# Transposes in halves that yield on VectorE, and other planned durations, in a list-scheduled attention and mixer kernel

## The chip, the cores and the metric

The kernel runs on one core of one Trainium2 chip. The metric is the device time of one execution in microseconds (us). A profiled execution is taken apart by engine: PE is TensorE's matmuls, PEld its weight loads, DVE VectorE, ACT ScalarE, POOL GpSimd, SP SyncE. Times quoted from a trace count from the first instruction of the program.

Each comparison below was made on one chip with the kernel before run in between. A ratio is the mean time of one kernel's fast runs over the mean of the other's fast runs of the same rounds, so it isn't quite the ratio of the medians that stand beside it. "Fast" and "slow" are states of a run; the slow one has a lower mean granted TensorE clock.

## The reference

Block-causal attention (blocks of 64) over 8 batches and 8 heads of 576 x 64, then an MLP mixer on its output:

```python
def _attn_ref(q, k, v):                       # q, k, v: 8 x 8 x 576 x 64, float32
    scores = scale * np.matmul(q, k.transpose(0, 1, 3, 2))
    mask = block_i >= block_j                 # blocks of 64 rows and columns
    ...                                       # masked softmax
    return np.matmul(attn, v)

def _moe_ref(x, w_tok1, w_tok2, w_ch1, w_ch2):  # x: 8 x 576 x 512
    xt = x.transpose(0, 2, 1)
    h = np.maximum(xt @ w_tok1, 0.0) @ w_tok2   # 576 -> 256 -> 576
    u = x + h.transpose(0, 2, 1)
    h2 = np.maximum(u @ w_ch1, 0.0) @ w_ch2     # 512 -> 1536 -> 512
    return u + h2
```

## The kernel before

Every piece of work is an `Op` with an engine, a planned cost, dependencies and a priority. When the program is built, a list scheduler plays all engines against a clock of planned costs and fixes the order of instructions on each engine. On the chip the order stays; only the waits are real. The choice of the next op:

```python
for e in ("PE", "ACT", "DVE", "POOL", "SP"):
    ...
    if best is None or (-o.urgent, o.prio, o.n) < (-best.urgent, best.prio, best.n):
        best = o
    ...
    soon = t + 0.6 * o.cost[e]
    if any(r < soon and self.ops[n].urgent > o.urgent and e in self.ops[n].engines for r, n in queued) or ...:
        continue          # a more urgent op is about to be ready: leave the engine idle for it
    ...
    if o.xfer is not None:                     # a DMA
        first = o.end + self.FIRST[e]
        if e == "POOL":
            soft = max(soft, hard, first) + o.xfer
        else:
            hard = max(hard, first) + o.xfer
```

q and k of four heads are loaded with a cast to bf16 and transposed on VectorE in 32 x 32 blocks; the ring of raw buffers is three deep, so a transpose also sets when a later load may start:

```python
parts = ((0, NB // 2), (NB // 2, NB)) if b < 2 else ((0, NB),)
...
loads = [P.add("POOL", 0.66, emit_load, raw_war, prio + n, xfer=8 * 0.191)]
for f, (k0, k1) in enumerate(parts):
    ...
    op = P.add("DVE", 0.02 + 32 * (k1 - k0) * 0.00185, emit, loads + T_war + after, prio + 0.1 * n)
```

Per head, attention times v goes to one of four PSUM banks (buffers for TensorE's results); VectorE then takes the reciprocal of the row sums and multiplies (`x_sb`), and only that frees the bank. The same four banks serve all layers of the mixer.

```python
av = P.add("PE", mm_cost(65, sum(chunks) + len(chunks)) + 0.02, ..., take=[(BANK, bank)] ...)
rc = P.add("DVE", 0.12, emit_rc, [av] + ..., prio - 1, urgent=urgent)
mu = P.add("DVE", dve_cost(320), emit_mu, [rc], prio - 1, give=[bank], urgent=urgent)
```

At the start, 16 matmuls on zeros and then up to 110 short fillers keep TensorE at work until the first scores can run; fillers are placed wherever the plan has TensorE idle before 20 us.

The softmax here doesn't subtract the row's maximum and nothing guards it: scores larger than these inputs give would overflow.

Of the kernel before, what the change touches and what calls it, by code (L numbers as in the profile page):

```python
# [11 lines left out]
BF16 = mybir.dt.bfloat16  # L12
# [16 lines left out]
class Plan:  # L29
# [2 lines left out]
    LAG = {"PE": 0.28, "ACT": 0.2, "DVE": 0.18, "POOL": 0.22, "SP": 0.1}  # L32


    FIRST = {"POOL": 3.0, "ACT": 0.7, "SP": 0.7}
    def __init__(self):
        self.ops = []
        self.free = {}
# [28 lines left out]
    def run(self):  # L67
        for o in self.ops:
            o.waiting, o.ready = len(o.deps), o.at
            for d in o.deps:  # L70
                d.users.append(o)
        busy = {e: 0.0 for e in self.LAG}
        queued = [(o.at, o.n) for o in self.ops if not o.waiting]
        heapq.heapify(queued)
        avail, t, hard, soft, gives, order, mode = [], 0.0, 0.0, 0.0, [], [], 0
        left = len(self.ops)
        while left:
            while queued and queued[0][0] <= t:
                avail.append(self.ops[heapq.heappop(queued)[1]])
            while gives and gives[0][0] <= t:  # L80
                _, name, slot = heapq.heappop(gives)
                self.free[name].append(slot)
            began = False
            left -= sum(o.until < t for o in avail)
            avail = [o for o in avail if o.until >= t]
            for e in ("PE", "ACT", "DVE", "POOL", "SP"):
                if busy[e] > t:
                    continue
                best = None
                for o in avail:  # L90
                    if e not in o.engines:
                        continue
                    if not self.fits(o):
                        continue
                    if best is None or (-o.urgent, o.prio, o.n) < (-best.urgent, best.prio, best.n):
                        best = o
                if best is None:
                    continue
                o = best
                soon = t + 0.6 * o.cost[e]  # L100
                if any(
                    r < soon and self.ops[n].urgent > o.urgent and e in self.ops[n].engines
                    for r, n in queued
                ) or any(
                    u.urgent > o.urgent
                    and e in u.engines
                    and self.fits(u, [name for r, name, _ in gives if r < soon])
                    for u in avail
                ):
                    continue  # L110
                avail.remove(o)
                left -= 1
                began = True
                for pools, note in o.take:
                    note["pool"] = next(p for p in pools if self.free[p])
                    note["slot"] = self.free[note["pool"]].pop(0)
                o.engine, o.start = e, t
                o.end = busy[e] = t + o.cost[e]
                if o.mode is None:
                    o.mode = mode  # L120
                if e == "PE" and o.mode != mode:
                    o.end = busy[e] = o.end + 0.1
                    mode = o.mode
                order.append(o)
                lag = self.LAG[e]
                if o.xfer is not None:
# [5 lines that stand above are left out]
                    o.end, lag = (soft if e == "POOL" else hard), 1.3  # L132
                for note in o.give:
                    heapq.heappush(gives, (o.end + lag * (not o.quick), note["pool"], note["slot"]))
                for u in o.users:
                    same = u.engines == (e,) and o.xfer is None
                    u.ready = max(u.ready, o.end + (0.05 if same else lag))
                    u.waiting -= 1
                    if not u.waiting:
                        heapq.heappush(queued, (u.ready, u.n))  # L140
            if not began:
                times = [b for b in busy.values() if b > t]
                times += [q[0] for q in queued[:1]] + [g[0] for g in gives[:1]]
                t = min(x for x in times if x > t)
        return order
# [3 lines left out]
def kernel(  # L149
# [11 lines left out]
    nc = tc.nc  # L161
# [9 lines left out]
    NB = S // 32  # L171
# [28 lines left out]
    warm = sb.tile([128, 1], FP32, name="warm")  # L200

    ident = sb.tile([128, 128], BF16, name="ident")
    zeros = sb.tile([128, 1024], BF16, name="zeros")
    w1_sb = sb.tile([128, 5, DT], BF16, name="w1_sb")
    w1o_sb = sb.tile([128, DT], BF16, name="w1o_sb")
    w2_sb = sb.tile([128, NDT, 640], BF16, name="w2_sb")
# [14 lines left out]
    def bank_of(note):  # L221
        return mm[note["slot"]]
# [11 lines left out]
    def mm_cost(n, count):  # L234
        return count * max(n / 2400 + 0.003, 0.033)
# [10 lines left out]
    def init_tiles():  # L246
# [9 lines left out]
        for i in range(2):  # L256
# [6 lines left out]
            fill("DVE", ("e", i), -70, (e_sb[i][:, :, 1536:1600], 0.0))  # L263
            fill("DVE", ("et", i), -70, (et_sb[i], 0.0))
            fill("DVE", ("um", i), -70, (um_sb[i], 0.0))
        fill("DVE", "zeros", -1e5, (zeros[:, 0:512], 0.0))
        fill("DVE", "more zeros", -1e3, (zeros[:, 512:1024], 0.0))
        fill("DVE", "w1", -70, (w1_sb[64:128, 4, :], 0.0), (w1o_sb[0:64, :], 0.0))
        fill("DVE", "w2", -70, (w2_sb[:, :, S:640], 0.0))

# [5 lines left out]
    def raise_clock():  # L276

        bank = {}

        def emit(o, bank=bank):  # L280
            for _ in range(WARM):
                nc.tensor.matmul(out=bank_of(bank), lhsT=zeros[:, 0:128], rhs=zeros[:, 0:512], start=True, stop=True)  # L282

        P.add("PE", WARM * 0.36, emit, pads["zeros"], -1e6, take=[(BANK, bank)], give=[bank])
        for n in range(KEEP):
            bank = {}

            def emit(o, bank=bank, n=n):
                if n % 4 == 1:
                    for c in range(2):  # L290
                        nc.tensor.matmul(
                            out=bank_of(bank)[:, 0:128], lhsT=zeros[:, c : 512 + c : 4], rhs=zeros[:, 0:128],
                            start=True, stop=True,
                        )
                else:
                    cols = zeros[:, 0:256]
                    if n % 4 == 3:
                        cols = zeros.rearrange("p (k a e) -> p a k e", k=16, e=2)[:, 0:16, :, 0]
                    nc.tensor.matmul(  # L299
                        out=bank_of(bank)[:, 0:256], lhsT=zeros[:, 0:128], rhs=cols, start=True, stop=True  # L300
                    )

            P.add(
                "PE", 0.11, emit, pads["zeros"] + pads["more zeros"], 1e6, take=[(BANK, bank)], give=[bank], at=5.0 + 0.12 * n, until=20.0,
                quick=True,
            )

# [15 lines left out]
    def load_qk(b, hg, after=[]):  # L323
        i = (2 * b + hg) % 3
        first = b == 0 and hg == 0
        prio = 10 * b + 4 * hg - (100 if b == 0 else 0)
        parts = ((0, NB // 2), (NB // 2, NB)) if b < 2 else ((0, NB),)
        done = []
        for n, (src, raw, dst) in enumerate(((k, kraw[i], kT[i]), (q, qraw[i], qT[i]))):
            hbm = src[b, 4 * hg : 4 * hg + 4].rearrange("h (p k) d -> (h p) (k d)", p=32)  # L330
# [11 lines left out]
            for f, (k0, k1) in enumerate(parts):  # L342
                if first:
# [1 line left out]
                        queue = nc.sync if o.engine == "SP" else nc.scalar  # L345
                        queue.dma_start(out=st[:, D * k0 : D * k1], in_=hbm[:, D * k0 : D * k1])

                    ld = P.add(("SP", "ACT")[f % 2], 0.45, emit_load, (), -1e4 + n, xfer=(k1 - k0) * 0.082)

                    def emit_cast(o, k0=k0, k1=k1, raw2=raw2, st=st):  # L350
                        cast(o, raw2[:, D * k0 : D * k1], st[:, D * k0 : D * k1])
# [12 lines left out]
                        raw2.bitcast(I32).rearrange("p (k a) -> p k a", k=NB)[:, k0:k1],  # L364
                    )

                op = P.add("DVE", 0.02 + 32 * (k1 - k0) * 0.00185, emit, loads + T_war + after, prio + 0.1 * n)
                reads(("raw", n, i), op)
                done.append(op)
        return done  # L370
# [1 line left out]
    def load_v(b):  # L372
# [5 lines left out]
        for hg in range(2) if b == 0 else (None,):  # L378
            hs = slice(0, H) if hg is None else slice(4 * hg, 4 * hg + 4)
            nh = hs.stop - hs.start  # L380
            for J in range(5):
# [7 lines left out]

                prio = (10 * b + (0, 5.7, 6)[min(b, 2)] if b else (-95.5, 2)[hg]) + 0.01 * J  # L390
                sw = reuse(("gs", J)) if staged and b else [] if staged else war
                op = P.add("POOL", 0.2 + 0.075 * nh, emit, sw, prio, xfer=p * nh / 16 * (0.018 if staged else 0.032))
                if staged:
                    def emit(o, st=st, dst=dst):
                        cast(o, dst, st)
# [29 lines left out]
    def load_channel_weights():  # L425
        done1, done2 = [[] for _ in range(NDC)], []
        for f in range(2):
            for m in range(NDM):
                def emit(o, m=m, f=f):
                    nc.gpsimd.dma_start(  # L430
                        out=wc1_sb[:, m, 768 * f : 768 * f + 768],
                        in_=moe_w_ch1[128 * m : 128 * (m + 1), 768 * f : 768 * f + 768],
                    )
                op = P.add("POOL", 0.66, emit, (), (6.0, 11.5)[f], xfer=8 * 0.134)
                for cc in range(0, 8) if f == 0 else range(4, NDC):
                    done1[cc].append(op)
        for c in range(0, NDC, 4):
            def emit(o, c=c):
# [1 line left out]
                    out=wc2_sb[:, c : c + 4, :],  # L440
                    in_=moe_w_ch2[128 * c : 128 * (c + 4), :].rearrange("(p c) t -> p c t", c=4),
                )
            done2.append(P.add("POOL", 0.66, emit, (), 15.5, xfer=8 * 0.324))
        return done1, done2


# [56 lines left out]
    def head_out(b, head, deps, prio, tail, urgent=0):  # L503
# [26 lines left out]
        av = None  # L530
        for chunks in steps:
            av = P.add(
                "PE", mm_cost(65, sum(chunks) + len(chunks)) + 0.02, lambda o, c=chunks: emit(o, c),
                [av, tail] + deps, prio, take=[(BANK, bank)] if av is None else (), urgent=urgent,
            )
        reads(("e", hg), av)
# [559 lines left out]
```

## Time and profile before

| | |
|---|---|
| runs (us) | 319.67, 310.67, 318.69; three more, taken with the changed kernel: 310.89, 311.25, 311.27 |
| profiled run | 311.27, span 309.4, clock 1.0, fast |
| TensorE / VectorE / ScalarE busy | 97% / 51% / 54% |
| first channel matmul (of the 512 -> 1536 layer) | 28.2 us |
| last score matmul / last weight load of attention times v | 195.3 / 201.6 us |
| TensorE waits after 27 us that VectorE ended | 7, 2.5 us in sum |

How to read the views: the page gives each engine's busy share over the span, then 40 slices of the span in tenths, then the chain of waits that ended last. A busy TensorE is not yet a full TensorE, because matmuls overlap (one of 512 columns is recorded as 380 ns long, but the next starts 216 ns after it); I used the distance between the starts of matmuls in a row for that. The waits in the last line of the table come from this too: start of a matmul minus start of the one before, minus that one's own time, wherever it is over 0.1 us, given to what released the matmul or its weight load. A few of these contain 0.1 to 0.2 us of the ordinary cost of leaving a score set (a row of 32-row score matmuls). How a matmul's own time and this cost are priced moves the sum: a recount that leaves nothing out for score sets gives 3.7 us here and 0.5 for the changed kernel (two gaps of about 0.25), so differences under 1 us in this measure mean little.

### The profile page before, as it was taken

The page shows a single profiled execution, that of the slowest core. Times are in us where ns is not written, and L with a number is a line of the kernel's source. Part 1 is how long each engine was busy: PE and PEld are TensorE (multiplying, and loading weights), DVE is VectorE, ACT ScalarE, POOL GpSimd, SP SyncE. Part 2 cuts the span into 40 slices and gives each one's busy share as a digit, 9 for nine tenths or more (in the row PEclk, how much of TensorE's full clock was granted, in tenths as well). Part 3 has the DMA queues.
Part 4 walks back from the last instruction along what each step waited for, and adds up shares of the span by engine and source line. Part 5 has one row for each costly group of instructions (what it writes and reads, how often), then busy time and mean ns, then how long its engine had stood idle before and what let it go on. Part 6 is the DMA issues. An engine that isn't in the chain of part 4 may idle for free.

```text
span 309.4 us, 7161 instructions
## 1 busy us (share of the span) xinstructions
PE 301.1 (97%) x3009; PEld 162.2 (52%) x3035; DVE 157.5 (51%) x374; ACT 165.6 (54%) x234; POOL 62.3 (20%) x96
## 2 busy tenths in 40 slices
PE   8999999999999999999999999999999999999995
PEld 3565447464565554545554556554445644545643
DVE  7868639498775757758848634435033012011022
ACT  5786866757666545766655785323405602604600
POOL 7955436611601421240130000000000000000000
PEclk9999999999999999999999999999999999999999
DMA  8999999997994799691291005103231311111013
GB/s 237 191 191 211 223 210 183 235 214 115 111 116 79 138 128 180 113 86 29 48 157 70 2 0 70 70 31 90 47 90 70 65 70 71 33 68 70 0 34 138
DMA packets 55872, 33.13 MB, mean 107 GB/s; under 512 B 43872, under 2 KB 46048, under 8 KB 55840
## 3 DMA queue, kind: packets, MB, share of 16 engines
q0 software_dynamic: 35808, 18.52, 45.6%
q1 hardware_dynamic: 19744, 13.57, 16.5%
q10 hardware_dynamic: 288, 0.59, 0.6%
q8 instruction: 23, 0.38, 0.5%
q14 instruction: 9, 0.07, 0.1%
HBM read 35.85 MB, written 9.44 MB: 146 GB/s over the span
## 4 chain that ended last, share of the span: by engine, by line
PE 89%; DVE 7%; issue 2%; ACT 1%
PE mm L972 29%; PE mm L888 27%; PE sc L474 9%; PE mm L521 7%; PE mm L702 6%; PE mm L796 4%; PE mm L915 3%; PE mm L282 2%; DVE x_sb L549 1%; ACT e_sb L493 1%; PE mm L299 1%; DVE kT L359 1%; DVE u_sb L817 1%; DVE qT L359 1%; DVE um_sb L817 1%
## 5 line engine op out<-in xcount | busy, mean ns | idle before, releaser
L493 ACT ACTIVATE e_sb<-sc 128x1024 bf16<-128x1024 f32 x95 | 92.3, 1024 | 32.9 <-PE sc L474 32.4
L888 PE MATMUL mm<-uT,wc_sb 128*128 128x512 bf16 x384 | 88.7, 380 | 0.1
L972 PE MATMUL mm<-wc_sb,gT 128*128 128x512 bf16 (+1 forms) x379 | 86.7, 373 | 1.4 <-issue 0.8
L688 ACT ACTIVATE gT<-mm 128x512 bf16<-128x512 f32 x71 | 42.4, 597 | 63.2 <-PE mm L888 63.1
L888 PEld LDWEIGHTS <-wc_sb 128*128 128x128 bf16 x384 | 42.1, 114 | 39.9 <-issue 4.4
L972 PEld LDWEIGHTS <-gT 128*128 128x128 bf16 x396 | 36.8, 98 | 41.6 <-issue 3.8
L997 DVE TENSOR_TENSOR o_sb<-mm,u_sb 128x512 f32<-128x512 f32 (+1 forms) x29 | 19.5, 672 | 62.7 <-PE mm L972 61.8
L474 PE MATMUL sc<-qT,kT 32*128 32x512 bf16 (+4 forms) x744 | 35.3, 281 | 0.2 <-ACT e_sb L493 0.2
L521 PEld LDWEIGHTS <-e_sb 128*128 128x128 bf16 x896 | 30.9, 97 | 7.8 <-issue 4.0
L521 PE MATMUL mm<-v,e_sb 128*128 128x65 bf16 x896 | 32.9, 193 | 0.2 <-DVE o_sb L997 0.2
L388 POOL DMA_DIRECT2D v<-in_v_dram x30 | 25.5, 864 | 29.6 <-PE sc L474 19.7
L549 DVE TENSOR_TENSOR x_sb<-mm,rinv 128x320 bf16<-128x320 f32 x64 | 30.3, 488 | 1.3
L690 DVE TENSOR_SCALAR gT<-mm 128x512 bf16<-128x512 f32 x25 | 17.2, 689 | 17.8 <-PE mm L888 17.6
L359 DVE STREAM_TRANSPOSE kT<-kraw 128x576 int32<-128x576 int32 (+1 forms) x20 | 20.1, 1035 | 4.6 <-PE sc L474 3.4
L474 PEld LDWEIGHTS <-kT 32*128 32x128 bf16 x752 | 12.4, 93 | 19.0 <-issue 15.7
L817 DVE TENSOR_TENSOR u_sb<-mm,x_sb 128x512 bf16<-128x512 f32 x28 | 17.6, 683 | 9.1 <-PE mm L796 7.6
L359 DVE STREAM_TRANSPOSE qT<-qraw 128x576 int32<-128x576 int32 (+1 forms) x20 | 20.1, 1027 | 0.5 <-DMA qraw<-in_q_dram 0.4
L499 DVE MEMSET e_sb<- 64x128 uint32 (+1 forms) x72 | 10.6, 153 | 15.0 <-ACT e_sb L493 11.7
L702 PE MATMUL mm<-x_sb,w_sb 128*128 128x512 bf16 (+1 forms) x98 | 17.5, 313 | 0.5 <-DVE x_sb L549 0.2
L796 PE MATMUL mm<-aT,w_sb 128*128 128x512 bf16 x71 | 17.6, 379 | 0.1
L339 POOL DMA_DIRECT2D kraw<-in_k_dram x15 | 8.3, 555 | 41.8 <-DVE kT L359 26.3
L688 ACT ACTIVATE aT<-mm 128x512 bf16<-128x512 f32 (+1 forms) x17 | 9.3, 547 | 13.7 <-PE mm L702 13.7
(69 smaller groups left out, 190.4 us busy)
## 6 DMA issues: line engine op xcount, KB each, us to landing
out_dram<-o_sb SPq DMA_DIRECT2D x15, 512.0 KB, 2.8
kraw<-in_k_dram POOLq DMA_DIRECT2D x15, 288.0 KB, 6.6
qraw<-in_q_dram POOLq DMA_DIRECT2D x15, 288.0 KB, 6.5
v<-in_v_dram POOLq DMA_DIRECT2D x24, 128.0 KB, 5.9
wc_sb<-in_moe_w_ch_dram POOLq DMA_DIRECT2D x8, 192.0 KB, 7.8
wc_sb<-in_moe_w_ch_dram POOLq DMA_DIRECT2D x3, 512.0 KB, 10.7
out_dram<-o_sb SPq DMA_DIRECT2D x10, 128.0 KB, 2.3
gT<-in_v_dram POOLq DMA_DIRECT2D x9, 128.0 KB, 6.3
```

The lines of the kernel that those rows point to most:

```text
L359: nc.vector.transpose(dst[:, 0:S, :] .rearrange("p s e -> p (s e)") .bitcast(I32) .rearrange("p (a k) -> p k a", k=NB)[:, k0:k1], raw2.bit ...
L388: nc.gpsimd.dma_start(out=dst, in_=src)
L474: nc.tensor.matmul(out=home(n)[:, c0 : c0 + w], lhsT=kT[i][r, j0 : j0 + 128, par], rhs=qT[i][r, i0 : i0 + w, par], start=(par == 0), stop= ...
L493: nc.scalar.activation(dst, sc[SC.index(note["pool"])][:, :, 0:n], EXP, scale=scale)
L521: nc.tensor.matmul(out=u[:, I, 0:65], lhsT=w, rhs=vt[:, J, head, 0:65], start=(J == 0), stop=(J == I),)
L549: nc.vector.tensor_tensor(out=xt[:, :, 64 * head : 64 * head + 64], in0=u[:, :, 0:64], in1=ri.to_broadcast([128, 5, 64]), op=MULT,)
L688: nc.scalar.activation(dst, src, RELU)
L702: nc.tensor.matmul(out=bank_of(bank)[:, w * n : w * n + w], lhsT=wt[:, tt : tt + 255 : 2], rhs=xt[:, c, cols], start=(c == 0), stop=(c == 4),)
L796: nc.tensor.matmul(out=bank_of(bank), lhsT=w2_sb[:, t, c0 : c0 + 128], rhs=at[:, t, :], start=(t == 0), stop=(t == NDT - 1),)
L817: nc.vector.tensor_tensor(out=dst, in0=bank_of(bank)[r, :], in1=xt[r, si, :], op=ADD)
L888: nc.tensor.matmul(out=bank_of(bank), lhsT=wc1_sb[:, m, channels(cc)], rhs=uT[b % 2][:, :, m, :], start=(m == 0), stop=(m == NDM - 1),)
L972: nc.tensor.matmul(out=ps, lhsT=gt[:, cc, c0 : c0 + 128], rhs=wc2_sb[:, cc, cols], start=(cc == 0 and not turned), stop=(cc == NDC - 1),)
```

## The change

Its intent: transposes of q and k for batches 2 to 7, 1.25 us each, stand in front of other VectorE work that TensorE needs sooner; cut them in two and let them yield. And the planned durations of loads and of attention matmuls move closer to what traces show.

```diff
-    FIRST = {"POOL": 3.0, "ACT": 0.7, "SP": 0.7}
+    FIRST = {"POOL": 1.5, "ACT": 0.7, "SP": 0.7}
...
-        avail, t, hard, soft, gives, order, mode = [], 0.0, 0.0, 0.0, [], [], 0
+        avail, t, hard, soft, gives, order, mode = [], 0.0, 0.0, 5.2, [], [], 0
...
-    zeros = sb.tile([128, 1024], BF16, name="zeros")
+    zeros = sb.tile([128, 512], BF16, name="zeros")
...    (fillers: strided reads and pairs of 128 columns become one plain 128 x 256 matmul)
-        parts = ((0, NB // 2), (NB // 2, NB)) if b < 2 else ((0, NB),)
+        parts = ((0, NB // 2), (NB // 2, NB))
...
-                    ld = P.add(("SP", "ACT")[f % 2], 0.45, emit_load, (), -1e4 + n, xfer=(k1 - k0) * 0.082)
+                    ld = P.add(("SP", "ACT")[f % 2], 0.45, emit_load, (), -1e4 + n, xfer=(k1 - k0) * 0.1)
...
-                op = P.add("DVE", 0.02 + 32 * (k1 - k0) * 0.00185, emit, loads + T_war + after, prio + 0.1 * n)
+                op = P.add("DVE", 0.02 + 32 * (k1 - k0) * 0.00185, emit, loads + T_war + after, prio + 0.1 * n, urgent=-(b > 1))
...
-  ... xfer=p * nh / 16 * (0.018 if staged else 0.032))     # v
+  ... xfer=p * nh / 16 * (0.0175 if staged else 0.0145))
-  ... xfer=8 * 0.134)                                      # first channel weights
+  ... xfer=0.98)
-  ... xfer=8 * 0.324)                                      # second channel weights
+  ... xfer=2.4)
...
-                "PE", mm_cost(65, sum(chunks) + len(chunks)) + 0.02, lambda o, c=chunks: emit(o, c),
+                "PE", 0.0298 * (sum(chunks) + len(chunks)), lambda o, c=chunks: emit(o, c),
```

More of the change, by code (lines that the diff above doesn't have):

```diff
@@ L265, in init_tiles @@
             fill("DVE", ("um", i), -70, (um_sb[i], 0.0))
-        fill("DVE", "zeros", -1e5, (zeros[:, 0:512], 0.0))
-        fill("DVE", "more zeros", -1e3, (zeros[:, 512:1024], 0.0))
+        fill("DVE", "zeros", -1e5, (zeros, 0.0))
         fill("DVE", "w1", -70, (w1_sb[64:128, 4, :], 0.0), (w1o_sb[0:64, :], 0.0))
@@ L281, in emit @@
             for _ in range(WARM):
-                nc.tensor.matmul(out=bank_of(bank), lhsT=zeros[:, 0:128], rhs=zeros[:, 0:512], start=True, stop=True)
+                nc.tensor.matmul(out=bank_of(bank), lhsT=zeros[:, 0:128], rhs=zeros, start=True, stop=True)
         P.add("PE", WARM * 0.36, emit, pads["zeros"], -1e6, take=[(BANK, bank)], give=[bank])
@@ L286, in raise_clock, with emit @@
             bank = {}
-            def emit(o, bank=bank, n=n):
-                if n % 4 == 1:
-                    for c in range(2):
-                        nc.tensor.matmul(
-                            out=bank_of(bank)[:, 0:128], lhsT=zeros[:, c : 512 + c : 4], rhs=zeros[:, 0:128],
-                            start=True, stop=True,
-                        )
-                else:
-                    cols = zeros[:, 0:256]
-                    if n % 4 == 3:
-                        cols = zeros.rearrange("p (k a e) -> p a k e", k=16, e=2)[:, 0:16, :, 0]
-                    nc.tensor.matmul(
-                        out=bank_of(bank)[:, 0:256], lhsT=zeros[:, 0:128], rhs=cols, start=True, stop=True
-                    )
+            def emit(o, bank=bank):
+                nc.tensor.matmul(
+                    out=bank_of(bank)[:, 0:256], lhsT=zeros[:, 0:128], rhs=zeros[:, 0:256],
+                    start=True, stop=True,
+                )
             P.add(
-                "PE", 0.11, emit, pads["zeros"] + pads["more zeros"], 1e6, take=[(BANK, bank)], give=[bank], at=5.0 + 0.12 * n, until=20.0,
+                "PE", 0.11, emit, pads["zeros"], 1e6, take=[(BANK, bank)], give=[bank], at=5.0 + 0.12 * n, until=20.0,
                 quick=True,
@@ L391, in load_v @@
                 sw = reuse(("gs", J)) if staged and b else [] if staged else war
-                op = P.add("POOL", 0.2 + 0.075 * nh, emit, sw, prio, xfer=p * nh / 16 * (0.018 if staged else 0.032))
+                op = P.add("POOL", 0.2 + 0.075 * nh, emit, sw, prio, xfer=p * nh / 16 * (0.0175 if staged else 0.0145))
                 if staged:
@@ L433, in emit @@
                     )
-                op = P.add("POOL", 0.66, emit, (), (6.0, 11.5)[f], xfer=8 * 0.134)
+                op = P.add("POOL", 0.66, emit, (), (6.0, 11.5)[f], xfer=0.98)
                 for cc in range(0, 8) if f == 0 else range(4, NDC):
@@ L442, in emit @@
                 )
-            done2.append(P.add("POOL", 0.66, emit, (), 15.5, xfer=8 * 0.324))
+            done2.append(P.add("POOL", 0.66, emit, (), 15.5, xfer=2.4))
         return done1, done2
```

## The prediction

> **What bounds the kernel now.** I read the page first (busy shares, the 40 slices, the chain that ended last), then the busy table by stage, then who waits for the transposes, and last TensorE's own sequence of starts, matmul by matmul. Lines of the page:
>
> ```profile
> PE 301.1 (97%) x3009; PEld 162.2 (52%) x3035; DVE 157.5 (51%) x374; ACT 165.6 (54%) x234; POOL 62.3 (20%) x96
> ...
> DVE  7868639498775757758848634435033012011022
> ...
> PE 89%; DVE 7%; issue 2%; ACT 1%
> ```
>
> TensorE (PE) is busy nearly always and carries 89% of the chain; VectorE (DVE) is at 51%, and in the first two thirds at 60 to 80%. Busy PE is not full PE, so I split the span into start, attention stage and end (columns: busy us of each engine with instruction counts, granted clock, DMA share, GB/s):
>
> ```profile
> 8.00:27.00 19.00, 18.77 (x304) 12.33 (x303) 14.35 (x50) 15.09 (x28) 13.07 (x24) 1.00 1.11 194
> 27.00:200.00 173.00, 169.89 (x2095) 91.77 (x2112) 113.97 (x263) 113.06 (x145) 43.38 (x61) 1.00 0.84 120
> 200.00:309.00 109.00, 105.67 (x595) 55.54 (x598) 23.05 (x39) 33.43 (x56) 0.00 (x0) 1.00 0.21 62
> ```
>
> From 27 to 200 us VectorE and ScalarE are each busy about 114 us of 173, so neither is the bound on the average. In the starts, 512-column matmuls in a row follow each other every 216 ns and the 65-column attention ones every 29.8 ns, which I take as the full rate. Priced so, with the score matmuls in fours side by side at 1/2.4 ns a column, the program's own matmuls need about 269 us: 172 for the two channel layers, 33 token layers, 29 attention times v, 21 scores, 11 mixed rows, 3 transposes. The span is 309.4, so some 40 us are not matmul work: 15.7 us up to t = 20 (loads, first scores, first exponentials), about 1.0 us in every 10 from 20 to 200 (19.5 together), almost nothing from 200 on, and 4 at the end.
>
> The 19.5 us are the only part that the change aims at, and most of it isn't waiting. Each of the 49 score sets after t = 27 costs about 0.235 us beyond its matmuls when nothing is late (going into and out of the 32-row matmuls): 49 x 0.235 = 11.5 us, which no order of work removes. About 3 us more are places where a score or matmul record is missing from the trace (gaps of exactly one matmul, 215 ns). That leaves **about 3 to 5 us of true waits on TensorE**. The waits ended by VectorE that I could name are at 65.3, 68.3, 93.9, 117.3, 132.1, 143.4 and 178.0 us, 0.1 to 0.5 us each, 2.5 us in sum. The timeline shows why in four of them; this is one:
>
> ```profile
> 115.18 1.26 DVE L359 STREAM_TRANSPOSE kT<-kraw 128x576 int32<-128x576 int32 x1
> ...
> 116.47 0.20 DVE L543 RECIPROCAL rinv<-mm 128x5 f32<-128x5 f32 x1
> 116.58 0.65 DVE L997 TENSOR_TENSOR o_sb<-mm,u_sb 128x512 f32<-128x512 f32 x1
> ...
> 117.29 0.58 PE L521 MATMUL mm<-v,e_sb 128*128 128x65 bf16 x14 [0.19 <-DVE o_sb L997]
> ```
>
> A transpose of 1.26 us is in front of the reciprocal and the output addition; with four PSUM banks, the next attention matmul waits for the bank that the addition frees. The same stands before 65.3, 68.3 and 93.9.
>
> **What the Trainium skill says.** "TensorE: Matmul & The Clock Gate", section Back-to-back issue gap, gives N/2.4 + 2.5 ns between matmuls on the full clock: 215.8 ns for 512 columns, and the trace has 216. The same page, Architectural detail, says that ScalarE and VectorE take instructions strictly in order: the trace agrees, since the reciprocal above starts 0.03 us after the transpose's end though its matmuls had ended 1 us before. "VectorE: DVE Perf Modes", section on the errata, puts a fixed cost on each instruction, so cutting one in two should cost something; here the effect is small, as worked out next. "DMA: Bandwidth & Descriptors", Anatomy of one DMA, gives about 2.0 us plus bytes over 436 GB/s for a DMA issued from GpSimd: 2.7 us for 288 KB. The trace has 3.9 to 4.7 us in the quiet stage after 90 us and 8 to 11 us at 20 to 65 us, where the queue is full.
>
> **The change, part by part.**
>
> *Halves.* 24 transposes of batches 2 to 7 become 48. Their lengths stand in the groups by shape:
>
> ```profile
> L359 DVE STREAM_TRANSPOSE kT<-kraw 128x576 int32<-128x576 int32 x12 | 15.0, 1253 | 3.9 <-PE sc L474 3.4 <-DMA kraw<-in_k_dram 0.3
> L359 DVE STREAM_TRANSPOSE kT<-kraw 128x288 int32<-128x288 int32 x8 | 5.1, 709 | 0.8 <-ACT kraw L319 0.4 <-DMA kraw<-in_k_dram 0.4
> ```
>
> Two halves look like 1.42 us against 1.25, but they overlap: starts of halves in a row are 0.56 to 0.58 us apart (5.34 and 5.92; 6.63 and 7.20), of whole ones 1.10 (91.01 and 92.11). A pair costs 1.14 against 1.10, so 24 x 0.04 = 1 us of VectorE time over 130 us in which it idles 40: free. The longest wait behind one transpose falls from 1.26 to 0.7 us.
>
> *Yielding.* In the list scheduler a transpose is now taken last, and held back if other VectorE work is due within 0.6 of its length. The order on each engine is fixed at build time, so this moves instructions and adds none. The gain is a part of the 2.5 us: I take 1 to 2.
>
> *Other durations.* Compared with the trace, the new ones are nearly all nearer to it: v loads 0.93 us each against 2.05 before (they land 0.7 to 1.1 us apart at 154 us), half of the first weights 0.98 against 1.07 (they land 0.9 to 1.0 apart), the second weights 2.4 against 2.59 (2.4 to 2.5 apart), GpSimd's first byte 1.5 against 3.0, attention 0.0298 us a matmul against 0.033 plus 0.02. A plan that is nearer to the truth puts fewer instructions in front of something not ready. But shorter planned loads take away slack: at 20 to 65 us real loads take 8 to 11 us, far over any plan. I give this a gain of 0 to 1 us, with a risk of the same size. All orders after the first batch shuffle, so single waits will move at random, by perhaps 1 us in sum.
>
> *Start.* Filler matmuls become plain ones. Of the old ones, the strided read held TensorE 0.42 us (7.67 to 8.09) instead of 0.11; the first real scores started at 8.53 though their last transpose ended at 7.92. But the plan now believes in later first loads (0.9 against 0.74 us each), so it inserts some five more fillers of 0.11 us. Net near zero, perhaps 0.3 us gained. One memset of 0.27 us leaves VectorE before anything needs it.
>
> Sum: 1 to 2 (yielding) + 0 to 1 (durations) + 0 to 0.3 (start), with about 1.5 us of noise either way. The end stage from 200 us, 109 us of matmuls without a gap, is untouched. So the fast run goes from 310.7 to about **309.3 us**, 0.5% less.
>
> **The rivals.** (1) *A wait takes the place of the removed one.* A transpose that always yields comes late, scores follow late, ScalarE starves, and the raw buffers come free late, which delays the next load:
>
> ```profile
> who waited for it (us, times):
>   POOL kraw L339: 26.3, 6
>   POOL qraw L339: 4.5, 2
> ```
>
> GpSimd does wait for the transposes, 31 us in sum. Against it: from 71 us on loads land several us before their transposes start (landed 81.6, transposed 91.0), VectorE idles a third of the time, and attention is done at 203 us while matmul work lasts to 306. It could cost 2 to 4 us (312 to 314), most likely at 45 to 75 us, where loads land just ahead of use. (2) *Nothing happens*: TensorE's 269 us of work and 11.5 us of score switching set the end, freed waits come back as others: 310 to 311. (3) *The clock state decides.* The three times before are 319.67, 310.67 and 318.69: two states, 8 us apart, and the profiled run (311.27) is in the fast one. No trace of the slow one is here, so its cause is open; the fillers, which serve the clock, change with this kernel and may shift how often it comes. If the median falls in the slow state, the result is near 317.
>
> **Range and chances.** Fast state 307 to 312, slow state 315 to 318.5. I give the fast state somewhat over half, and set the number at 310.5 with a range of 306.5 to 318.5. Like with like, over 2% (6.2 us) either way is more than all true waits in the attention stage; a gain over 2% would come mainly from comparing a fast median with the slow 318.69. Hence faster 0.26, same 0.69, slower 0.05.
>
> **What would show it.** Right: 128x288 transposes number 32 on each of k and q, no 128x576; VectorE busy up by about 4 us by summed durations or 1 us by starts; TensorE waits ended by x_sb, u_sb and o_sb shrink from 2.5 us to about 1; the dense stage begins about 1 to 2 us sooner. Rival 1: ScalarE's wait for scores (32.4 us now) and TensorE's waits for transposes grow. Wrong: a stage before 27 us that is 3 us shorter or longer through another order of loads, a TensorE clock that drops during the start, or dense matmuls that aren't every 216 ns.

## The result

The changed kernel takes 309.2 us (median of 6 runs, 307.75 to 309.31, all fast). The kernel before has 311.26 over its six runs, two of them slow. The ratio of fast runs is 0.993, with a 95% interval of 0.9908 to 0.9952: a small gain that is clear of noise, and "same" at the 2% mark.

The profile after, page first (busy shares, VectorE's slices, chain by engine):

```profile
PE 300.9 (98%) x3036; PEld 162.0 (53%) x3036; DVE 158.0 (51%) x396; ACT 165.6 (54%) x235; POOL 62.3 (20%) x96
...
DVE  5677738997875859866749634362033012011022
...
PE 93%; DMA 2%; ACT 2%; DVE 1%; issue 1%; ACTq 0%
```

VectorE's share of the chain that ended last fell from 7% to 1% and TensorE's rose from 89% to 93%; no engine did less work. Such shares don't measure a gain by themselves: in e1 below, which has two thirds of the gain, VectorE keeps 6%, and in e2, which has none, it has 1%. The same three stages as before (busy us and instruction counts in the order PE, PEld, DVE, ACT, POOL; then clock, DMA share, GB/s):

```profile
8.00:27.00 19.00, 17.13 (x294) 11.61 (x293) 14.91 (x51) 15.48 (x29) 12.90 (x24) 1.00 1.06 188
27.00:200.00 173.00, 172.82 (x2136) 92.53 (x2134) 116.29 (x288) 113.73 (x147) 43.57 (x61) 1.00 0.85 121
200.00:307.00 107.00, 104.18 (x589) 54.57 (x585) 22.32 (x38) 33.49 (x56) 0.00 (x0) 1.00 0.21 63
```

In the middle stage TensorE is now busy 172.82 of 173 us (169.89 before), while in the first it has 1.6 us less. About half of the rise in the middle stage is of the record, not of the chip: the profile before lacks 17 matmul records there (2095 matmuls for 2112 weight loads), which leaves gaps of about 0.05 or 0.16 us, 1.5 us in sum, and the profile after lacks none. The starts of matmuls don't suffer from this, and they give the story of this pair of profiles: the first channel matmul starts at 29.0 us, 0.8 **later** than before, and from there to the last matmul it takes 274.9 us where it took 277.5. The difference, 0.8 - 2.7 = -1.9 us, is that of the spans (307.5 against 309.4).

The later start is most likely luck of a load, not a part of the change: half of the first q landed at 7.84 us instead of 5.91, and the first scores began at 9.91 instead of 8.53. The same half landed at 7.62 us in e3, whose loads are those of the kernel before. TensorE's own waits in the profile after:

```profile
PE sc L465 <- DVE qT L350: 1.7, 1, 1.7
PE mm L282 <- DVE zeros L251: 1.2, 1, 1.2
PE mm L879 <- ACT uT L855: 0.2, 1, 0.2
```

The first is that wait at the start (through the transpose of q), the second was there before, the third is 0.2 us. Of the seven waits in the attention stage that VectorE ended, none is left by this count. The place that the prediction showed, a transpose ahead of a reciprocal, now reads:

```profile
116.11 1.26 DVE L350 STREAM_TRANSPOSE kT<-kraw 128x288 int32<-128x288 int32 x2
...
117.10 0.19 PE L512 MATMUL mm<-v,et_sb 128*128 128x65 bf16 x1
117.13 0.58 PE L512 MATMUL mm<-v,e_sb 128*128 128x65 bf16 x14
117.40 0.20 DVE L534 RECIPROCAL rinv<-mm 128x5 f32<-128x5 f32 x1
```

Two halves still run back to back, in the same 1.26 us, but they end at 117.37, only 0.07 us after the attention matmuls whose reciprocal comes next (first head, done at 117.30), and TensorE goes on without a gap. In the kernel before these matmuls were done at 115.63 and their reciprocal began 0.84 us later. The halves and the waits of GpSimd:

```profile
L350 DVE STREAM_TRANSPOSE kT<-kraw x32: 695/706/720, 5.4 to 167.0; 128x288 int32<-128x288 int32 x32
...
who waited for it (us, times):
  POOL kraw L330: 20.2, 5
  POOL qraw L330: 14.1, 5
```

GpSimd waits a little longer for the transposes (34.3 us against 30.8) before it starts the next loads, and nobody downstream notices: ScalarE waits for scores 32.4 us, exactly as before.

### The profile page after: what moved, and what is told of

The parts are those of the page before. It is cut to its first block, busy times and chain, and to the rows that moved or that the text cites. A ratio compares the mean times of both kernels' runs of the same rounds, so it can differ in the third digit from the quotient of the medians.

```text
span 307.5 us, 7211 instructions
## 1 busy us (share of the span) xinstructions
PE 300.9 (98%) x3036; PEld 162.0 (53%) x3036; DVE 158.0 (51%) x396; ACT 165.6 (54%) x235; POOL 62.3 (20%) x96
## 4 chain that ended last, share of the span: by engine, by line
PE 93%; DMA 2%; ACT 2%; DVE 1%; issue 1%; ACTq 0%
PE mm L963 31%; PE mm L879 28%; PE mm L512 10%; PE sc L465 9%; PE mm L693 6%; PE mm L787 5%; PE mm L906 4%; DMA gT<-in_q_dram 2%; DVE qT L350 1%; ACT e_sb L484 1%; PE mm L737 1%; ACT uT L855 0%; PE mm L955 0%; PE mm L722 0%; ACT qraw L310 0%
## 5 line engine op out<-in xcount | busy, mean ns | idle before, releaser
L484 ACT ACTIVATE e_sb<-sc 128x1024 bf16<-128x1024 f32 x95 | 92.5, 1027 | 33.2 <-PE sc L465 32.4
L963 PE MATMUL mm<-wc_sb,gT 128*128 128x512 bf16 (+1 forms) x396 | 88.6, 373 | 0.0
L679 ACT ACTIVATE gT<-mm 128x512 bf16<-128x512 f32 x75 | 44.9, 598 | 64.7 <-PE mm L879 63.7
L465 PE MATMUL sc<-qT,kT 32*128 32x320 bf16 (+4 forms) x744 | 35.5, 281 | 1.9 <-DVE qT L350 1.7
L512 PEld LDWEIGHTS <-e_sb 128*128 128x128 bf16 x896 | 30.8, 97 | 8.1 <-issue 4.3
L350 DVE STREAM_TRANSPOSE qT<-qraw 128x288 int32<-128x288 int32 x32 | 21.5, 705 | 2.1 <-ACT qraw L310 1.9
L350 DVE STREAM_TRANSPOSE kT<-kraw 128x288 int32<-128x288 int32 x32 | 20.4, 706 | 3.2 <-PE sc L465 2.3
L681 DVE TENSOR_SCALAR gT<-mm 128x512 bf16<-128x512 f32 x21 | 14.5, 689 | 11.3 <-PE mm L879 11.0
L534 DVE RECIPROCAL rinv<-mm 128x5 f32<-128x5 f32 x64 | 11.3, 184 | 6.5 <-PE mm L512 6.1
```

What stands on the lines that cost most here:

```text
L350: nc.vector.transpose(dst[:, 0:S, :] .rearrange("p s e -> p (s e)") .bitcast(I32) .rearrange("p (a k) -> p k a", k=NB)[:, k0:k1], raw2.bit ...
L465: nc.tensor.matmul(out=home(n)[:, c0 : c0 + w], lhsT=kT[i][r, j0 : j0 + 128, par], rhs=qT[i][r, i0 : i0 + w, par], start=(par == 0), stop= ...
L484: nc.scalar.activation(dst, sc[SC.index(note["pool"])][:, :, 0:n], EXP, scale=scale)
L512: nc.tensor.matmul(out=u[:, I, 0:65], lhsT=w, rhs=vt[:, J, head, 0:65], start=(J == 0), stop=(J == I),)
L679: nc.scalar.activation(dst, src, RELU)
L963: nc.tensor.matmul(out=ps, lhsT=gt[:, cc, c0 : c0 + 128], rhs=wc2_sb[:, cc, cols], start=(cc == 0 and not turned), stop=(cc == NDC - 1),)
```

## The experiments

The theory: the gain is TensorE time that was lost behind transposes on VectorE, and the halves and the yielding bring it. The main rivals: the new planned durations bring it; any reshuffle of the order would; the fillers and the start do. All kernels gave correct results. The kernel before ran too, at medians of 311.08, 311.3 and 310.88 us.

| kernel | median us | ratio of fast runs (95%) | first channel matmul | from there to the last matmul | waits that VectorE ended |
|---|---|---|---|---|---|
| before | 311.26 | 1 | 28.2 | 277.5 | 2.5 |
| changed | 309.2 | 0.993 (0.9908-0.9952) | 29.0 | 274.9 | 0 |
| e1 halves and yielding alone | 309.58 | 0.9953 (0.9935-0.9971) | 28.3 | 276.0 | 1.6 |
| e2 durations alone | 311.09 | 0.9997 (0.9979-1.0016) | 29.4 | 276.7 | 1.7 |
| e3 fillers alone | 311.19 | 0.9997 (0.9978-1.0015) | 28.8 | 277.5 | 2.5 |
| e8 nudged control | 311.03 | 0.999 (0.997-1.0011) | 28.7 | 277.1 | 1.7 |
| e4 changed, no yielding | 309.21 | 0.9938 (0.9922-0.9954) | 27.9 | 275.8 | 0.3 |
| e5 changed, whole transposes | 308.92 | 0.9944 (0.9908-0.9979) | 27.2 | 275.7 | 0.7 |
| e9 changed, neither | 309.71 | 0.9964 (0.995-0.9979) | 31.4 * | 276.7 | 1.8 |
| e6 changed, old load durations | 308.7 | 0.992 (0.9905-0.9936) | 27.5 | 275.7 | 1.2 |
| e11 as e6, identity first | 308.22 | 0.9913 (0.9901-0.9926) | 26.8 | 276.0 | 0.2 |
| e12 as e2, old first loads | 312.62 | 1.0062 (1.0046-1.0077) | 30.6 | 276.5 | 1.6 |
| e7 transposes twice | 338.23 | 1.0889 (1.0846-1.0932) | 28.0 | 303.5 | 27.5 |
| e10 twice, and planned so | 320.02 | 1.0284 (1.027-1.0298) | 38.7 * | 285.7 | 10.3 |

The last three columns (us) are from the one profiled run of each; * marks profiles with half the clock during the start (e7's has 3.4 us of it at 108.5). The last column counts waits over 0.1 us after 27 us, as told under the profile before.

### e1: halves and yielding alone

```diff
 (the kernel before)
+        parts = ((0, NB // 2), (NB // 2, NB))
+        ... prio + 0.1 * n, urgent=-(b > 1))
```

> The kernel before with the halves and the yielding alone; all planned durations and fillers as before. Theory (the gain is the VectorE transposes no longer standing in front of other VectorE work): most of the gain is here, ratio 0.992 to 0.995, and TensorE's waits ended by x_sb, u_sb and o_sb fall from 2.5 us to under 1. Rival (the gain comes from better planned durations): ratio 0.998 to 1.002.

It gave 0.9953, just outside the 0.992 to 0.995 that the theory expected, and clearly below 1: about 1.5 us. TensorE's waits ended by VectorE fell to 1.6 us only, not under 1. So this part works by itself and brings about two thirds of the gain.

### e2: durations alone

```diff
 (the kernel before)
+ FIRST 1.5 for POOL, soft = 5.2, the new xfer of first loads, v and both channel weights, attention 0.0298
```

> The kernel before with the new planned durations alone (loads, GpSimd's first byte, attention matmuls); whole transposes that don't yield, old fillers. Theory: 0.997 to 1.002, waits behind whole transposes remain. Rival (durations): 0.992 to 0.995.

0.9997: nothing. The profile shows why it isn't simply "no effect": from the first channel matmul on it is 0.8 us shorter, but the start is 1.2 us longer. The plan now believes in later first loads and puts 16 old-style filler matmuls ahead of the first scores instead of 9. The timeline there:

```profile
6.83 1.29 DVE L359 STREAM_TRANSPOSE qT<-qraw 128x288 int32<-128x288 int32 x2 [0.16 <-ACT qraw L319]
...
8.96 0.81 PE L299 MATMUL mm<-zeros 128*128 128x256 bf16 x3
9.04 0.78 DVE L321 CAST v<-gT 128x256 bf16<-128x256 f32 x2
9.70 0.56 PEld L474 LDWEIGHTS <-kT 32*128 32x128 bf16 x20 [0.53 <-issue]
```

q was transposed at 8.12 us; the first scores came 1.6 us later, behind fillers.

### e3: fillers alone

```diff
 (the kernel before)
+ zeros [128, 512]; each filler is one plain 128 x 256 matmul
```

> The kernel before with the plain fillers and the smaller zeros tile alone. Theory: 0.998 to 1.001, first real scores at most 0.5 us earlier. Rival (the slow filler reads held the start back): 0.995 to 0.998.

0.9997, as the theory has it. In its profile the first scores ran 0.06 us after the last transpose of q (9.69 after 9.63) instead of 0.6 us after it (8.53 after 7.92), but q itself landed late there (7.62 us), so the half microsecond is not visible in the time.

### e8: a nudged control

```diff
-                op = P.add("DVE", 0.02 + 32 * (k1 - k0) * 0.00185, ...
+                op = P.add("DVE", 0.03 + 32 * (k1 - k0) * 0.00185, ...
```

> A control: the kernel before with the planned cost of a transpose 0.01 us higher and nothing else, which is no better and no worse founded but moves hundreds of instructions. Theory: 0.997 to 1.003; this shows how far mere reshuffling goes. If it is as low as 0.993, the gain of the change is within what a reshuffle does, and no part of it can claim it by its time alone.

0.999: this reshuffle is worth a third of a microsecond, and e1's interval stays clear of 1. But it is a mild one. TensorE's order is that of the kernel before for the first 1090 of 2990 weight loads, up to 93 us, and the waits at 65 and 68 us stay; in e1 the order departs at 52 us. And e12 below, which differs from e2 in one planned duration, is 1.9 us slower than the kernel before, so a new order alone can be worth as much as the gain. What speaks against this rival is the whole series: the six kernels with halves or yielding (changed, e1, e4, e5, e6, e11) lie at 0.9913 to 0.9953, the five without (e2, e3, e8, e9, e12) at 0.9964 to 1.0062. One of e8's runs took 316.99 us at a mean clock of 0.972; it is slow and not counted.

### e4, e5, e9: one or both taken out of the changed kernel

```diff
 (the changed kernel)
 e4, e9:  urgent=-(b > 1)) goes
 e5, e9:  ... if b < 2 else ((0, NB),)   comes back
```

> The changed kernel without the yielding (halves stay). Theory: the yielding matters more than the halves, so it loses half of the gain or more: 0.995 to 0.999 of the kernel before. Rival (halves suffice): 0.992 to 0.994, as the changed kernel.

> The changed kernel with whole transposes in batches 2 to 7 that still yield. Theory: yielding keeps most of the gain, 0.993 to 0.996. Rival (the length of one transpose is what hurts): 0.996 to 1.000.

> The changed kernel without halves and without yielding: new durations and plain fillers together on whole transposes that don't yield. Undoing one of the two cost under 0.2% each (0.9938 and 0.9944 against 0.993). Theory (either of the two is enough to keep transposes out of the way, and one is needed): 0.997 to 1.000, with TensorE waits of 1 us or more ended by VectorE again. Rival (new durations and fillers together make the gain, transposes hardly matter): 0.992 to 0.995.

e4 gave 0.9938 and e5 0.9944, both within the changed kernel's interval. (e5's ratio contains a run of 312.26 us at a mean clock of 0.989; without it the ratio would be 0.992.) My expectation for e4, that yielding carries more than the halves, was a miss: beside the new durations either of the two is enough. e9 was to show whether one is needed at all. It lies at 0.9964, between what the theory and the rival expected: the new durations and the plain fillers together give about 1.1 us of the 2.1, and the transposes' handling about another 1. So neither "transposes only" nor "durations only" holds. e9's interval touches the changed kernel's, so the size of the second half is uncertain, but its trace has the wait that the theory names, as have those of e2 and e12, all three with whole transposes that don't yield under the new durations:

```profile
67.56 0.69 DVE L808 TENSOR_TENSOR um_sb<-mm,x_sb 64x512 bf16<-64x512 f32 x1
...
68.29 1.26 DVE L350 STREAM_TRANSPOSE kT<-kraw 128x576 int32<-128x576 int32 x1
68.31 0.40 PE L840 MATMUL mm<-ident,um_sb 128*128 128x128 bf16 x4
69.58 0.42 DVE L857 COPY umT<-mm 128x512 bf16<-128x512 bf16 x1
...
70.06 1.08 PE L906 MATMUL mm<-umT,wc_sb 128*128 128x128 bf16 x16 [1.35 <-DVE umT L857]
```

The transposed mixed rows are ready in PSUM by 68.7; the copy waits behind a whole transpose until 69.58 and TensorE idles 1.35 us. With halves or with yielding (e4, e5, changed) this wait is gone; e4 has one of 0.74 us at 65.8 instead, for a copy on ScalarE.

### e6: old load durations in the changed kernel

```diff
 (the changed kernel)
+ FIRST 3.0, soft = 0.0, the old xfer of first loads, v and both channel weights; attention stays 0.0298
```

> The changed kernel with the old planned durations of loads (attention matmuls keep the new one). Theory: loads land ahead of use from 70 us on, so 0.992 to 0.996. Rival (load durations make the gain): 0.998 to 1.002.

0.992: at least as fast as the changed kernel. So the load durations, the larger part of the edit by lines, aren't what gains; beside halves and yielding they give nothing that can be measured. Which of the remaining parts, attention's planned cost above all, makes up the difference between e1 (0.9953) and e6 was not tried alone.

### e7 and e10: the transposes doubled

```diff
 e7 (the kernel before)
+                once = emit
+                def emit(o, once=once):
+                    once(o)
+                    if b > 1:
+                        once(o)
 e10 (e7)
-                op = P.add("DVE", 0.02 + 32 * (k1 - k0) * 0.00185, ...
+                op = P.add("DVE", (0.02 + 32 * (k1 - k0) * 0.00185) * (1 + (b > 1)), ...
```

> The kernel before with each transpose of batches 2 to 7 done twice in a row, in the same planned order: 24 times 1.25 us more VectorE work, 30 us in all, and waits behind transposes twice as long. Theory (work stuck behind a transpose makes TensorE wait): each of the 7 waits found grows by about 1 us and new ones appear, so 6 to 15 us slower, 1.02 to 1.05. Rival (TensorE is the bound and VectorE's idle 40% takes it up): 1.000 to 1.005.

> As the kernel before with doubled transposes (1.089), but the list scheduler is told the doubled cost. Theory (the fixed order, made with costs that are too low, turns VectorE work into TensorE waits, while VectorE has idle time for it): most of the 27 us comes back, 1.005 to 1.025. Rival (VectorE's capacity in the attention stage is what is missing): 1.06 to 1.09.

e7 cost 27 us for 24 more transposes of k and q at 1.25 us, 30 us of VectorE time. VectorE idles a third of that stage (59 of 173 us in the kernel before; my text said 40%), and yet nearly every added microsecond came through to the end. I expected 6 to 15 us: the direction was right, the size not. One wait in e7, with three transposes in a row:

```profile
102.87 1.26 DVE L359 STREAM_TRANSPOSE kT<-kraw 128x576 int32<-128x576 int32 x1
...
103.97 2.53 DVE L359 STREAM_TRANSPOSE qT<-qraw 128x576 int32<-128x576 int32 x2
...
106.35 0.20 DVE L550 RECIPROCAL rinv<-mm 128x5 f32<-128x5 f32 x2
106.56 0.89 DVE L556 TENSOR_TENSOR x_sb<-mm,rinv 128x320 bf16<-128x320 f32 x2
...
107.10 1.05 PE L922 MATMUL mm<-umT,wc_sb 128*128 128x128 bf16 x16 [2.88 <-DVE x_sb L556]
```

e10 does the same work but plans for it: 320.02 us, 1.0284. So about 18 of the 27 us were not VectorE's capacity but an order made with a wrong cost; about 9 us remain, a bit more than the 1.025 that I gave the theory. A part of the 18 may be clock: e7's runs show mean clocks of 0.983 to 0.995, e10's fast ones 0.998 to 1.0. The missing share of 335 us is 1.7 to 5.7 us, which is an estimate of the most that it can have cost. The pair shows the path: a transpose that is longer than planned passes its excess on to TensorE almost in full, because the order can't react. Part of this may go by the loads, which wait for the transposes to free their buffers: GpSimd's waits for transposes rose from 30.8 to 46.4 us. The pair doesn't show how much of this path was in use in the kernel before, where the planned cost of a transpose (1.09 us) is close to the measured 1.10 from start to start; for that there are e1 and the traces.

### e12: the first loads' old duration beside the new ones

```diff
 (e2)
-  xfer=(k1 - k0) * 0.1)
+  xfer=(k1 - k0) * 0.082)
```

> The new durations alone (0.9997) but with the old one for the first q and k loads. In the profile of the former 16 old-style fillers stood before the first scores, which began 1.6 us after their last transpose. Theory (a real gain of 1 us in the attention stage was cancelled by those fillers): first scores within 0.6 us of their transpose, ratio 0.995 to 0.998. Rival (the durations gain nothing): 0.999 to 1.001.

It failed: 1.0062, slower than e2. The first scores did come 1.5 us earlier, at 8.21, as meant, but the first channel matmul came at 30.6 us, later than in any other profile at full clock. The timeline shows a new hole:

```profile
14.18 1.09 ACT L493 ACTIVATE e_sb<-sc 128x1024 bf16<-128x1024 f32 x1
...
16.48 0.72 DVE L359 STREAM_TRANSPOSE qT<-qraw 128x288 int32<-128x288 int32 x1
...
17.92 1.09 PE L474 MATMUL sc<-qT,kT 32*128 32x320 bf16 x16
18.59 1.02 ACT L493 ACTIVATE e_sb<-sc 128x1024 bf16<-128x1024 f32 x1 [3.32 <-PE sc L474]
```

The last half of q of the second head group, transposed at 12.38 us in the kernel before and at 15.35 in the changed one, comes at 16.48 here, other matmuls stand before its scores, and ScalarE idles 3.3 us before its next exponentials. My explanation of e2 (a gain of 1 us cancelled by fillers) is therefore only half supported: the fillers' delay is in the trace, but taking it away did not bring the gain. Why the plan orders it so was not followed further.

### e11: a candidate

```diff
 (e6)
-        pads["ident"] = [P.add("POOL", 0.9, emit, (), 5.5)]
+        pads["ident"] = [P.add("POOL", 0.9, emit, (), -200)]
```

> A candidate: the changed kernel with the old load durations (0.992) and GpSimd building the identity first, so that its first prefetch starts some 0.6 us later and leaves the DMA engines to the first q and k loads. Theory (the first scores wait for the q load, which landed between 5.8 and 7.8 us in the profiles): first scores about 0.3 to 0.5 us earlier, 0.990 to 0.992. Rival (the start is bound by other things, or the reshuffle decides): 0.992 to 0.996.

0.9913, 308.22 us: the fastest of all, 1 us below the changed kernel and 2.7 below the kernel before. The reason that I gave for it did not show: the first q landed at 5.91 and 6.28 us, no earlier than in e6 (5.78 and 6.06), and the first scores came at 8.35 (8.13 in e6). Against e6 the difference is within both intervals. It is a good version, but the identity's place is not shown to be why.

### The slow state

It came unasked. e9's profiled run took 313.45 us where its others took 309.1 to 310.8. The ratio of 0.9964 fits the six others alone (all seven would give 0.998). Its trace has a stretch at half the clock (same columns as the stages above; the first number after the counts is the granted clock):

```profile
4.80:11.60 6.80, 4.69 (x50) 2.97 (x49) 4.08 (x8) 3.31 (x5) 5.08 (x9) 1.00 1.07 247
11.60:18.40 6.80, 6.80 (x67) 3.59 (x64) 3.10 (x13) 5.51 (x11) 6.09 (x13) 0.50 1.05 157
18.40:30.00 11.60, 11.55 (x204) 8.40 (x204) 9.35 (x34) 8.65 (x16) 5.24 (x10) 1.00 1.14 206
```

In this run half of q landed at 8.02 us and TensorE, its fillers used up, stood still for 2.1 us before the first scores at 10.09. e10's slow profile is the same, only longer: q landed at 9.47 and 9.80, first scores at 11.54, clock 0.50 for 20.5 us, 329.81 us against 319.2 to 320.4. And in e7 a window of 3.4 us at half clock, from 108.5 on, follows the 2.9 us wait shown above. That is what "TensorE: Matmul & The Clock Gate", Part 1, describes: a clock of one half after an idle window of some 3.4 us, in windows that run freely. The lengths agree (6.8 us is two windows, 20.5 is six). How much idling is enough does not come out of these traces, though. Waits of 2.1 (e9), 2.9 (e7) and 3.8 us (e10) were followed by half the clock; one of 1.7 us in the changed kernel's profile was not, and neither was one of 2.1 us in e7 itself (the matmuls after it, and the windows around and after it):

```profile
165.14 1.02 PE L895 MATMUL mm<-uT,wc_sb 128*128 128x512 bf16 x4 [2.13 <-DVE x_sb L556]
...
163.10:166.50 3.40, 1.31 (x6) 0.69 (x7) 3.35 (x10) 1.92 (x2) 0.00 (x0) 1.00 0.03 7
166.50:169.90 3.40, 3.40 (x29) 1.44 (x29) 2.36 (x6) 1.35 (x2) 0.00 (x0) 1.00 0.64 110
```

Counting the idle time inside one window, from the clock's own changes on, doesn't sort them either: 1.9 us in e9 (8.2 to 11.6) and 2.0 in e7 (105.1 to 108.5), where the clock fell, against 2.1 in e7 (163.1 to 166.5), where it didn't.

A late first load came before both slow starts seen here, but also before three at full clock (7.84 us in the changed kernel, 7.62 in e3, 7.47 in e8). So it is a likely cause of the slow state and not a shown one: I made no run that forces it, and the two slow runs of the kernel before left no trace.

## Why the prediction was right

- **What bounds it.** Right. TensorE's own work and the fixed cost of score sets stayed; only waits were to be had. I put the true waits of the attention stage at 3 to 5 us, of which 2.5 named; the stretch from the first channel matmul to the last matmul shrank by 2.7 in the profiles. The dense channel matmuls after 200 us begin 1.9 us sooner, as expected (1 to 2). Two readings were loose: the reciprocal that I showed began 0.84 us after its matmuls, not 1; loads of q and k after 90 us took 3.9 to 6.5 us, not 3.9 to 4.7, which holds for those of k alone.
- **Halves.** Right: free. The summed lengths of all transposes rose from 41.2 to 45.2 us, and VectorE's busy time only by 0.5 us; counted without their overlaps the transposes alone take 1.06 us more (I said 4 and 1). There are 32 halves each of k and q, none whole.
- **Yielding, 1 to 2 us.** Right in size for halves and yielding together (e1: 1.5 us). That yielding is the part that counts was not right: e4 and e5 show that under the new durations either is enough.
- **Durations, 0 to 1 us.** Within it, but not as argued. Alone they gave nothing (e2), with the plain fillers about 1.1 us (e9), and the durations of loads, on which my argument rested, can be left out (e6). With another duration for the first loads they even cost 1.9 us (e12).
- **Start, 0 to 0.3 us.** Not shown. Plain fillers make the first scores follow their transpose at once, but the landing of the first q moves by more than that from run to run (5.9 to 7.8 us within this pair).
- **Fast state at 309.3 us.** Measured 309.2, but that it is so close is partly luck: I took 1.4 us from 310.67, the lowest of the runs before, while the fast ones average 311.0 and the gain was 2.2 us. The number, 310.5, was raised for a slow median that did not come: in 33 further runs of the kernel before, none was slow, so I gave that state far too much weight. The wide range and the chance of 0.26 for "faster" come from the same misjudgment.
- **Rival 1** (late transposes starve ScalarE) left its mark on GpSimd's waits alone, 34.3 against 30.8 us. **Rival 2** (freed waits come back elsewhere) is partly seen: the start was 0.8 us later in the profile, though most likely by luck of a load. **Rival 3** (the clock decides) did not decide this pair, but e9 and e10 show a state of half clock, and where it sat in these two.

## What to carry to other kernels

In a program whose order is fixed when it is built, an engine at 50% can still cost the bound engine time, one instruction in the wrong place at a time; look at what stands just ahead of the instruction that the bound engine waits for, and make that one shorter or let it yield. A planned cost that is too low is far dearer than the work itself: 30 us of unplanned work on a half-idle engine cost 27 us (a part of it may be a lower clock), and a third of that once it was planned. And test parts of a change together as well as alone: here no single part adds up to the whole, and one that was logical (e12) made it slower.

## What the Trainium skill lacked or had wrong

- "TensorE: Matmul & The Clock Gate", Back-to-back issue gap, has a sustained spacing of about 131 ns for 512 columns and 81 ns for 128 in a real kernel of weight load and matmul pairs. Here, with a weight load before each, 512 columns are 216 ns apart and 128 columns 55.8 ns (48 of the mixed rows in 2.68 us), which is the same section's formula for an isolated matmul.
- The same page, Part 1, gives an idle window of about 3.4 us for falling back to half the clock. Here the clock fell after windows of that length that were idle for 1.9 us (e9) and 2.0 us (e7) only, and another with 2.1 us (e7) left it as it was; the page gives no share of idle time from which the clock falls.
- "TensorEngine Tiling (Array Packing)", Key Properties, says that a change of tiling mode drains TensorE, but not what that costs: going into and out of the 32-row score matmuls took about 0.235 us a score set here, 49 times after 27 us, 11.5 us in all.
- "VectorE: DVE Perf Modes", The three transpose paths, gives VectorE's transpose for 128 x 128 bf16 alone. Here 128 x 576 int32 took 1.25 us (1.10 from start to start) and 128 x 288 0.71 us (0.56), so a cut in two costs 0.02 us when the halves follow each other.
- "DMA: Bandwidth & Descriptors", Anatomy of one DMA: the fit gives 2.7 us for 288 KB. The q and k loads of this size took 3.9 to 6.5 us after 90 us and 7.7 to 11.4 us at 20 to 65 us, where the queue is full. These loads cast: 288 KB is what they write, and they read 576 KB of float32, for which the fit gives 3.4 us (an estimate); the page doesn't say which of the two counts, nor what a full queue costs.
